# One-core attention and token-routing kernel: the first pair's preparation moved ahead of the constants, and one batch's second layer moved into the tail

## The chip, the cores and the metric

The kernel runs on one core of one Trainium2 chip. The metric is the time of one execution on the device in microseconds (us). Within the core, TensorE (PE in the profile, with its weight loads as PEld), VectorE (DVE), ScalarE (ACT) and GpSimd (POOL) each work through their own list of instructions in order, and SyncE (SP) issues most of the DMAs. They meet through semaphores only.

## The reference

```python
# attention: B, H, S, D = 8, 8, 1152, 64, all float32
q_pool = q.reshape(B, H, S // 2, 2, D).mean(axis=3)
scores = np.matmul(q_pool, k.transpose(0, 1, 3, 2)) / np.sqrt(D)
attn = softmax(scores)                     # with 1e-9 added to the sum
x = np.matmul(attn, v)                     # bridged to (8, 576, 512)
# mixture of depths: capacity 128, w1 (512, 1024), w2 (1024, 512)
s = np.einsum('bsd,d->bs', x, w_gate)
for b in range(B):
    top = np.argpartition(-s[b], capacity)[:capacity]
    y = np.maximum(x[b, top] @ w1, 0.0) @ w2
    out[b] = x[b];  out[b, top] += sigmoid(s[b, top])[:, None] * y
```

## The kernel before

The work is cut into 32 **pairs** of heads (8 batches of 4 pairs) and each pair into two **halves** of 288 pooled queries. For a half, `scores` multiplies nine chunks of 128 keys with the queries: four 64x64-tiled matmuls a chunk (L817), then one exponential of 128x576 on ScalarE (L824). `weighted` multiplies the exponentials with the values (L835, 36 matmuls); `folded` sums them (three additions on GpSimd, L856, and two transposing reductions on VectorE, L861). A float32 matmul is two passes in the trace, so 36 matmuls are 72 rows.

`run` (L1292) writes the order out by hand; the program is built in that order, engine by engine, with no scheduler to move anything. In iteration h the scores of half h are issued, then the weighted sum of half h-1, then one step of every routing unit that is under way (`units`, L1286). A **routing unit** is a generator, `routed` (L996), one for each batch. Each `yield True` ends its step for this iteration. Its steps are: the batch's scores to one line, the ranks (L1076 to L1110), the list of chosen tokens, the gather of 128 rows from the output (L1177, an indirect DMA on GpSimd), their transposition (L1191, L1194), the **first layer** (L1202, 32 matmuls of 128x128, two ReLU copies at L1210), and the **second layer** (L1215, 8 matmuls of 128x512), after which the rows are scaled (L1235), added (L1238) and scattered back (L1239). The tile `xe` (L1176), the index and the gates have two buffers; the PSUM pool has four.

After the loop comes the **tail** (L1365 to L1393). The last batch but one (`old`) has its first and second layer left, and the last batch (`new`) everything from its line of scores on. For the last batch the line comes from a matmul with a diagonal (L1042, L1052, L1059), the columns of scores from five tiny transposes (L679, L682), and the chosen tokens from ten small passes (L1146). The tail interleaves the two by `pieces(unit, n)`: n further steps of a generator.

At the **head** (L1298 to L1305) the first pair is loaded in its natural layout: its queries in two DMAs on ScalarE's queue (L755), its first three chunks of keys in two DMAs on SP's (L759), then the other six chunks and the values. `constants` (L602) runs 12 matmuls of ones on TensorE (L612) and builds the tables: on GpSimd the iotas (L628 to L639), on VectorE four operations (L630, L634, L642, L650). `prepare_first` (L765) adds neighbouring queries (L776, one head on VectorE, one on GpSimd), transposes three chunks of keys (L783, copied by ScalarE at L788), the queries (L794, two copies on VectorE at L801), then the other six chunks (copied by ScalarE). Then the second pair is loaded, and the loop begins.

Of the kernel before, what the change touches and what calls it, by code (L numbers as in the profile page):

```python
# [10 lines left out]
P = 128  # L11
BLK = 32

G = 3
# [520 lines left out]
class _Plain:  # L535
# [10 lines left out]
    def __init__(self, ctx, tc, q, k, v, moe_w_gate, moe_w1, moe_w2, capacity, out):  # L546
        self.tc, self.nc = tc, tc.nc
        self.q, self.k, self.v, self.out = q, k, v, out
        self.w_gate_in, self.w1_in, self.w2_in = moe_w_gate, moe_w1, moe_w2
        B, H, S, D = q.shape  # L550
        self.B, self.H, self.S, self.D = B, H, S, D
        self.Sp = S // 2
        self.Dm = H * D
        self.F = moe_w1.shape[1]
        self.NC = S // P
        self.NPAIR = H // 2
        self.HALF = self.Sp // 2
        self.QB = self.Sp // BLK
        self.HB = self.HALF // BLK
        self.KB = S // BLK  # L560
        self.NF = self.Sp // P
        self.TAIL = self.Sp - self.NF * P
        self.NT = self.NF + 1
        self.ND = self.Dm // P
        self.NFC = self.F // P
        self.NG = self.NC // G
        self.scale = 0.5 / math.sqrt(D)
        self.slots = [(s, min(P, capacity - s)) for s in range(0, capacity, P)]
# [7 lines left out]
        assert all(w > 1 for _, w in self.slots) and capacity < self.Sp  # L576
# [12 lines left out]

        self.sums = self.const.tile([P, self.B * self.NPAIR, self.QB], F32, name="sums")  # L590
        self.w_gate = self.const.tile([P, self.NPAIR, BLK], F32, name="w_gate")
        self.w1 = self.const.tile([P, self.ND, self.F], F32, name="w1")
        self.w2 = self.const.tile([P, self.NFC, self.Dm], F32, name="w2")
# [8 lines left out]
    def constants(self):  # L602
        nc, const = self.nc, self.const
        self.ones = const.tile([P, P], F32, name="ones")
        nc.gpsimd.memset(self.ones[:, :], 1.0)
# [2 lines left out]
        nc.scalar.activation(once[:, :], self.ones[0:1, 0:1], AF.Exp)  # L608

        ps = self.banks()[:, 0, 0:P]  # L610
        for _ in range(12):
            nc.tensor.matmul(ps, lhsT=self.ones[:, :], rhs=self.ones[:, :], start=True, stop=True)  # L612
        self.ident = const.tile([P, P], F32, name="ident")
        make_identity(nc, self.ident[:, :])

        self.before = const.tile([P, P], F32, name="before")
        nc.gpsimd.memset(self.before[:, :], 1.0)
# [38 lines left out]
    def tokens(self):  # L656
        nc = self.nc
# [107 lines left out]
    def prepare_first(self, pair):  # L765

        nc, NC, D = self.nc, self.NC, self.D
        kT = pair["kT"] = self.load.tile([P, self.S], F32, name="kT")
        qT = pair["qT"] = self.load.tile([P, self.Sp], F32, name="qT")
        rows, third = 3 * BLK, self.QB // 3  # L770
        acc = self.work.tile([P, G, 2 * self.HALF], F32, name="acc")
        qp = acc.rearrange("p u n -> p (u n)")[0:rows, 0 : 2 * third * D]
        qp = qp.rearrange("p (n j d) -> p n j d", j=2, d=D)
        of = pair["q"].rearrange("p j (n r) d -> p n j r d", r=2)
        for j, engine in enumerate((nc.vector, nc.gpsimd)):
            engine.tensor_tensor(  # L776
                out=qp[:, :, j, :], in0=of[:, :, j, 0, :], in1=of[:, :, j, 1, :], op=ALU.add
            )

        def keys(a, z):  # L780
            ps = self.banks().rearrange("p b n -> p (b n)")
            for c in range(a, z):
                nc.tensor.transpose(  # L783
                    ps[:, (c - a) * P : (c - a + 1) * P],
                    pair["k"][:, c, :, :].rearrange("p j d -> p (j d)"),
                    self.ident[:, :],
                )
            nc.scalar.copy(kT[:, a * P : z * P], ps[:, 0 : (z - a) * P])  # L788

        keys(0, G)  # L790
        ps = self.banks()
        per = third // 2
        for n in range(third):
            nc.tensor.transpose(  # L794
                ps[:, n // per, n % per * rows : (n % per + 1) * rows],
                qp[:, n, :, :].rearrange("p j d -> p (j d)"),
                self.ident[0:rows, 0:rows],
            )
        to = qT.rearrange("p (t b n i) -> p b n i t", t=3, b=2, i=BLK)
        for bank in range(2):  # L800
            nc.vector.tensor_copy(  # L801
                to[:, bank], ps[:, bank, 0 : per * rows].rearrange("p (n i t) -> p n i t", n=per, t=3)
            )
        keys(G, NC)

    def scores(self, half):

        nc, pair, n = self.nc, half["pair"], self.HALF
        qs = slice(half["s"] * n, (half["s"] + 1) * n)
# [1 line left out]
        for c in range(self.NC):  # L811
            sc = self.banks()
            for e in range(2):
                keys = slice(e * self.D, (e + 1) * self.D)
                for j in range(2):
# [6 lines left out]
                        stop=True,  # L822
                    )
            nc.scalar.activation(p[:, c // G, c % G, :, :], sc[:, :, 0:n], AF.Exp, scale=self.scale)  # L824

    def weighted(self, half):

# [144 lines left out]
    def gated(self, half):  # L972
# [6 lines left out]
        if half["s"] == 1:  # L979
            nc.vector.tensor_tensor(  # L980
                out=pair["part"][:, pair["hp"], :],
                in0=pair["red"][:, :],
                in1=pair["rec"][:, :],
                op=ALU.mult,
            )
            if pair["hp"] == self.NPAIR - 1:
                unit = self.routed(pair["b"], pair["part"])
                next(unit)
                self.routing.append(unit)

# [5 lines left out]
    def routed(self, b, part):  # L996
# [134 lines left out]
        for s0, w in self.slots:  # L1131
# [66 lines left out]
            for f0 in range(0, self.NFC, 4):  # L1198
                pv = self.banks()[:, 0, :].rearrange("p (c n) -> p c n", n=P)
                for f in range(4):  # L1200
# [7 lines left out]
                        )  # L1208
                    if f == 3:
                        nc.scalar.activation(hT[:, f0 : f0 + 4, 0:w], pv[:, :, 0:w], AF.Relu)  # L1210
                    yield f0 + f == self.NFC - 1

            ps = self.banks()[:, 0, :]
            for f in range(self.NFC):
# [4 lines left out]
                    start=(f == 0),  # L1219
                    stop=(f == self.NFC - 1),  # L1220
                )
                if f < self.NFC - 1:
                    yield False
            if b == self.B - 1:
                nc.vector.scalar_tensor_tensor(  # L1225
                    out=xe[0:w, :],
# [58 lines left out]

    def units(self):  # L1286

        for unit in self.routing[::-1]:
            if not any(unit):
                self.routing.remove(unit)  # L1290

    def run(self):  # L1292
        nc = self.nc
        pairs = [(b, hp) for b in range(self.B) for hp in range(self.NPAIR)]
        n_halves = 2 * len(pairs)
        halves = []
        self.routing = []
        upcoming = self.load_first(*pairs[0])  # L1298
        self.load_gate()
        self.constants()  # L1300
        self.prepare_first(upcoming)
        self.tokens()
        loaded = self.load_pair(*pairs[1]) if len(pairs) > 1 else None
        if loaded:
            self.load_values(loaded)  # L1305
        weights = self.weight_loads()
        for h in range(n_halves + 1):
            if h < n_halves:
# [14 lines left out]
                    next(weights, None)  # L1323
                half = {"pair": pair, "s": s}
                halves.append(half)
                self.scores(half)
                if h > 1:

                    of = halves[h - 2 - s]["pair"]
# [36 lines left out]


        self.gated(halves[-1])
        new = self.routing.pop()
        old = self.routing.pop() if self.routing else iter(())  # L1370

        def pieces(unit, n):
            for _ in range(n):
                next(unit, None)

        pieces(old, 4)
        pieces(new, 1)
        pieces(old, 1)
        pieces(new, 1)
        pieces(old, self.NFC - 5)  # L1380
        pieces(new, 2)
        pieces(old, self.NFC // 2)
        pieces(new, 1)
        low = self.counted()
        pieces(old, self.NFC)
        for unit in self.routing + [old]:
            for _ in unit:
                pass
        pieces(new, 1)
        count = self.outside(low)  # L1390
        for _ in new:
            pass
        return nc.values_load(count[0:1, 0:1])  # L1393


# [1 line left out]
def kernel(  # L1397
# [12 lines left out]


    args = (q, k, v, moe_w_gate, moe_w1, moe_w2, capacity, out)
    if capacity % P == 1:

        _any_scores(tc, *args)
        return
# [38 lines left out]
```

## Time and profile before

| | |
|---|---|
| median of 4 runs | 715.04 us |
| the four runs | 713.64, 714.69, 715.39, 716.05 us |
| the profiled execution | 715.53 us, its span 713.6 us |
| TensorE busy in the span | 701.4 us (98%) |
| mean granted TensorE clock | 0.995 |
| longest waits of TensorE in the waits view | 1.4 us (L1052), 1.0 (L612), 0.7 (L1146), 0.7 (L817), 0.7 (L1202) |

The profile is of one execution. Its span runs from the first to the last instruction; 1.9 us of the execution's own time lie around it. A line of the timeline view gives the start in us from the span's start, the time it covers, the engine, the line of the kernel, the operation, the tiles written and read, the size, how many instructions were merged, and in brackets how long the engine had been idle before them and what ended that. The windows view gives, for one stretch, its length, each engine's busy time (with the number of instructions) and the mean granted TensorE clock.

### The profile page before, as it was taken

Reading aid. Unit: us, or ns where it says so; the run is one execution under the profiler, and the core shown is the slowest. Engines: PE = TensorE matmul, PEld = TensorE weight load, DVE = VectorE, ACT = ScalarE, POOL = GpSimd, SP = SyncE. Lnnn points to the kernel's source line nnn. Section 1 sums busy time; section 2 is a strip of 40 time slices with the busy share of each in tenths; the row PEclk is TensorE's granted clock in tenths of the full one; section 3 lists DMA queues with packets and bytes.
Section 4 is the critical chain, followed back from the end, with each engine's and each line's share of the span. In section 5 each row is a group of like instructions: output and inputs, shape, how many; then the busy total and the mean of one; then the engine's idle time right before and its main releaser. Section 6 shows DMA issues by size and latency. Waiting matters only on the chain. (4 is left out here: it accounts for less than half of the span.)

```text
span 713.6 us, 23393 instructions
## 1 busy us (share of the span) xinstructions
PE 701.4 (98%) x9952; PEld 495.8 (69%) x9952; DVE 495.0 (69%) x792; ACT 443.5 (62%) x962; POOL 485.8 (68%) x453
## 2 busy tenths in 40 slices
PE   8999999999999999999999999999999999999896
PEld 6668887875857767576677967678675676756654
DVE  4877777896549965498754978459773697758540
ACT  5677777777547774577746775477754777547310
POOL 5777777868568695577955788467784877657620
PEclk9999999999999999999999999999999999999999
DMA  8899876769682495726866278742878337622200
GB/s 172 180 185 182 178 154 119 132 129 157 123 160 53 89 174 104 138 51 128 156 114 107 51 149 139 133 84 52 165 127 146 68 87 135 119 42 61 51 23 27
DMA packets 389490, 82.86 MB, mean 116 GB/s; under 512 B 376640, under 2 KB 376640, under 8 KB 389376
## 3 DMA queue, kind: packets, MB, share of 16 engines
q1 hardware_dynamic: 387872, 76.49, 57.3%
q0 software_dynamic: 1280, 4.20, 1.8%
q8 instruction: 80, 1.31, 0.8%
q10 hardware_dynamic: 224, 0.59, 0.3%
q14 instruction: 34, 0.28, 0.1%
HBM read 69.65 MB, written 11.59 MB: 114 GB/s over the span
## 5 line engine op out<-in xcount | busy, mean ns | idle before, releaser
L824 ACT ACTIVATE p<-ps 128x576 f32<-128x576 f32 x576 | 319.4, 690 | 3.0 <-PE ps L817 2.4
L856 POOL TENSOR_TENSOR acc<-p 128x576 f32<-128x576 f32 x192 | 266.0, 1414 | 55.1 <-ACT p L824 49.8
L817 PE MATMUL ps<-qT,kT 64*64 64x288 f32 x4608 | 297.2, 406 | 0.9 <-DVE qT L801 0.7
L835 PE MATMUL ps<-p,v_sb 64*64 64x288 f32 x4608 | 294.4, 403 | 0.3 <-ACT p L824 0.2
L835 PEld LDWEIGHTS ps<-p,v_sb 64*64 64x64 f32 x4608 | 210.4, 133 | 71.8 <-ACT p L824 15.9
L817 PEld LDWEIGHTS ps<-qT,kT 64*64 64x64 f32 x4608 | 190.4, 132 | 95.0 <-ACT p L824 27.1
L861 DVE TRANSPOSE_TENSOR_REDUCE fold<-p 128x54 f32<-128x1728 f32 x64 | 126.1, 1970 | 129.6 <-ACT p L824 129.6
L861 DVE TRANSPOSE_TENSOR_REDUCE fold<-acc 128x54 f32<-128x1728 f32 x64 | 124.8, 1950 | 40.4 <-POOL acc L856 40.4
L843 ACT COPY two<-ps 128x576 f32<-128x576 f32 x64 | 40.9, 639 | 130.1 <-PE ps L835 111.2
L845 POOL TENSOR_TENSOR av<-two 128x288 f32<-128x288 f32 x64 | 51.2, 799 | 30.5 <-ACT two L843 28.9
L955 POOL TENSOR_TENSOR x<-avb,rec 128x576 f32<-128x576 f32 x32 | 37.0, 1157 | 41.6 <-DVE rec L953 24.2
L1202 PEld LDWEIGHTS ps<-xeT,w 128*128 128x128 f32 x512 | 58.0, 192 | 3.7 <-ACT sums L901 2.2
L1202 PE MATMUL ps<-xeT,w 128*128 128x128 f32 x512 | 59.7, 277 | 0.7 <-ACT xeT L1194 0.7
L1215 PE MATMUL ps<-w,hT 128*128 128x512 f32 x128 | 58.8, 612 | 0.0
L924 POOL TENSOR_TENSOR prod<-avb,w_gate 128x288 f32<-128x288 f32 x64 | 51.3, 802 | 0.6 <-DVE avb L914 0.6
L901 ACT ACTIVATE sums<-total,tiny 32x18 f32<-32x18 f32 x124 | 38.1, 308 | 11.9 <-DVE total L892 10.3
L1215 PEld LDWEIGHTS ps<-w,hT 128*128 128x128 f32 x128 | 24.2, 194 | 30.1 <-issue 30.1
L732 POOL TENSOR_TENSOR qp<-qb 128x576 f32<-128x576 f32 x31 | 43.7, 1411 | 1.6 <-DMA qb<-in_q_dram 1.6
L735 DVE STREAM_TRANSPOSE kT<-kb 128x1152 f32<-128x1152 f32 x31 | 42.5, 1370 | 0.0
L1210 ACT ACTIVATE hT<-ps 128x512 f32<-128x512 f32 x16 | 9.6, 597 | 48.7 <-PE ps L1202 48.7
L1238 POOL TENSOR_TENSOR xe<-y,xe 128x512 f32<-128x512 f32 x7 | 8.9, 1271 | 42.0 <-ACT y L1235 42.0
L914 DVE STREAM_TRANSPOSE avb<-av 128x288 f32<-128x288 f32 x64 | 29.2, 457 | 7.9 <-POOL av L845 7.8
(94 smaller groups left out, 330.2 us busy)
## 6 DMA issues: line engine op xcount, KB each, us to landing
kb<-in_k_dram SPq DMA_DIRECT2D x124, 144.0 KB, 3.6
qb<-in_q_dram SPq DMA_DIRECT2D x124, 144.0 KB, 3.8
v_sb<-in_v_dram SPq DMA_DIRECT2D x124, 144.0 KB, 3.5
out_dram<-x SPq DMA_DIRECT2D x128, 72.0 KB, 2.9
lines<-row_rank SPq DMA_DIRECT2D x7, 640.0 KB
w<-in_moe_w_dram SPq DMA_DIRECT2D x8, 512.0 KB, 5.4
sc_row<-row SPq DMA_DIRECT2D x7, 288.0 KB
acc<-in_q_dram ACTq DMA_DIRECT2D x2, 288.0 KB
```

The source lines that it names most:

```text
L732: nc.gpsimd.tensor_tensor(out=qp[:, :, :], in0=pair["q"][:, :, 0, :], in1=pair["q"][:, :, 1, :], op=ALU.add)
L735: nc.vector.transpose(kT.rearrange("p (c g i) -> p c g i", c=self.NC, i=BLK), pair["k"].rearrange("p (g c) d -> p c g d", c=self.NC),)
L817: nc.tensor.matmul(sc[keys, j, 0:n], lhsT=pair["kT"][rows, c * P + keys.start : c * P + keys.stop], rhs=pair["qT"][rows, qs], start=True, ...
L824: nc.scalar.activation(p[:, c // G, c % G, :, :], sc[:, :, 0:n], AF.Exp, scale=self.scale)
L835: nc.tensor.matmul(av[j * self.D : (j + 1) * self.D, e, 0:n], lhsT=half["pair"]["v"][keys, j, c, :], rhs=half["p"][keys, c // G, c % G, j, :],
L843: nc.scalar.copy(two[:, :, :], av[:, :, 0:n])
L845: nc.gpsimd.tensor_tensor(out=half["av"][:, :], in0=two[:, 0, :], in1=two[:, 1, :], op=ALU.add)
L856: nc.gpsimd.tensor_tensor(out=acc[:, u, :], in0=units[:, 0, u, :], in1=units[:, 1, u, :], op=ALU.add)
L861: nc.vector.tensor_reduce(fold[:, a, :], of.rearrange("p u (m d) -> p (u m) d", d=BLK), AX.X, ALU.add, apply_transpose=True,)
L924: self.nc.gpsimd.tensor_tensor(out=pair["prod"][:, ns, :], in0=pair["avb"][:, ns, :], in1=self.w_gate[:, hp : hp + 1, :].broadcast_to([P, ...
L1202: nc.tensor.matmul(pv[:, f, 0:w], lhsT=self.w1[:, c, (f0 + f) * P : (f0 + f + 1) * P], rhs=xeT[:, c, 0:w], start=(c == 0), stop=(c == self ...
L1215: nc.tensor.matmul(ps[0:w, 0 : self.Dm], lhsT=hT[:, f, 0:w], rhs=self.w2[:, f, :], start=(f == 0), stop=(f == self.NFC - 1),)
```

## The change

The change has two parts that do not touch each other.

At the **head**, `constants` is split. `first_constants` keeps the matrix of ones, the warm-up matmuls (10 in place of 12) and the identity; `prepare_first` now follows it directly, and the other constants follow that. Both additions of queries go to VectorE. The two copies of transposed queries go to VectorE and ScalarE, one each. The transposes of the last six chunks of keys are no longer issued in `prepare_first`: they are returned as `rest` and issued behind the first chunk of scores, with their copy on VectorE instead of ScalarE. The gate's four DMAs (`load_gate`) go behind the loads of the second pair.

In the **tail**, the unit of the last batch but two is stopped after its first layer (the mark `"hidden"`), and its second layer, `older`, is issued in the tail: six matmuls ahead of the last batch's diagonal matmuls, two behind them. The order of what was there changes with it: the last batch's ranks and pick now stand ahead of all of `old`'s first layer, and `old`'s second layer is cut in five and three matmuls around the transposition of the last batch's rows.

```diff
@@ first_constants / constants
-        for _ in range(12):
+        for _ in range(10):
             nc.tensor.matmul(ps, lhsT=self.ones[:, :], rhs=self.ones[:, :], start=True, stop=True)
         self.ident = const.tile([P, P], F32, name="ident")
         make_identity(nc, self.ident[:, :])
+
+    def constants(self):
+        nc, const = self.nc, self.const
@@ prepare_first
-        for j, engine in enumerate((nc.vector, nc.gpsimd)):
-            engine.tensor_tensor(
+        for j in range(2):
+            nc.vector.tensor_tensor(
...
-        def keys(a, z):
+        def keys(a, z, copy):
...
-            nc.scalar.copy(kT[:, a * P : z * P], ps[:, 0 : (z - a) * P])
-        keys(0, G)
+            copy(kT[:, a * P : z * P], ps[:, 0 : (z - a) * P])
+        keys(0, G, nc.scalar.copy)
...
-        for bank in range(2):
-            nc.vector.tensor_copy(
+        for bank, copy in enumerate((nc.vector.tensor_copy, nc.scalar.copy)):
+            copy(
                 to[:, bank], ps[:, bank, 0 : per * rows].rearrange("p (n i t) -> p n i t", n=per, t=3)
             )
-        keys(G, NC)
+        return lambda: keys(G, NC, nc.vector.tensor_copy)
@@ scores
             nc.scalar.activation(p[:, c // G, c % G, :, :], sc[:, :, 0:n], AF.Exp, scale=self.scale)
+            if c == 0 and behind_first:
+                behind_first()
@@ routed
-                    yield f0 + f == self.NFC - 1
+                    yield "hidden" if f0 + f == self.NFC - 1 else False
...
-                if f < self.NFC - 1:
-                    yield False
+                yield False
@@ units
-        for unit in self.routing[::-1]:
-            if not any(unit):
-                self.routing.remove(unit)
+        for entry in self.routing[::-1]:
+            b, unit = entry
+            if b in self.waiting:
+                continue
+            end = next((mark for mark in unit if mark), None)
+            if end is None:
+                self.routing.remove(entry)
+            elif end == "hidden" and b == self.B - 3:
+                self.waiting.add(b)
@@ run
         upcoming = self.load_first(*pairs[0])
-        self.load_gate()
-        self.constants()
-        self.prepare_first(upcoming)
-        self.tokens()
+        self.first_constants()
+        rest = self.prepare_first(upcoming)
+        self.constants()
         loaded = self.load_pair(*pairs[1]) if len(pairs) > 1 else None
         if loaded:
             self.load_values(loaded)
+        self.load_gate()
...
-                self.scores(half)
+                self.scores(half, rest if h == 0 else None)
...
-        pieces(old, 4)
-        pieces(new, 1)
-        pieces(old, 1)
-        pieces(new, 1)
-        pieces(old, self.NFC - 5)
-        pieces(new, 2)
-        pieces(old, self.NFC // 2)
+        pieces(older, self.NFC - 2)
+        pieces(new, 1)
+        pieces(older, 2)
+        pieces(new, 3)
+        pieces(older)
+        pieces(old, self.NFC)
         pieces(new, 1)
         low = self.counted()
-        pieces(old, self.NFC)
-        for unit in self.routing + [old]:
-            for _ in unit:
-                pass
-        pieces(new, 1)
+        pieces(old, self.NFC - 3)
+        pieces(new, 2)
+        pieces(old)
         count = self.outside(low)
-        for _ in new:
-            pass
+        pieces(new)
```

The rest of the diff changes the handling of other capacities, which the inputs do not use.

More of the change, by code (lines that the diff above doesn't have):

```diff
@@ L567, in __init__ @@
         self.scale = 0.5 / math.sqrt(D)
-        self.slots = [(s, min(P, capacity - s)) for s in range(0, capacity, P)]
+        self.slots = [(0, capacity)]
         assert tuple(out.shape) == (B, self.Sp, self.Dm)
@@ L575, in __init__ @@
         assert self.F == self.NFC * P and self.NFC % 4 == 0
-        assert all(w > 1 for _, w in self.slots) and capacity < self.Sp
+        assert 1 < capacity <= P
         def pool(name, bufs, **kw):
@@ L600, in quarters, with first_constants @@
                 yield j, slice(e * BLK, (e + 1) * BLK), slice(at, at + BLK)
-    def constants(self):
+    def first_constants(self):
         nc, const = self.nc, self.const
@@ L654, in constants @@
         nc.gpsimd.memset(self.tiny[:, :], 1e-9)
-    def tokens(self):
-        nc = self.nc
         self.meta = self.const.tile([P, self.NT, 2], F32, name="meta")
@@ L799, in prepare_first, with scores @@
         to = qT.rearrange("p (t b n i) -> p b n i t", t=3, b=2, i=BLK)
-        for bank in range(2):
-            nc.vector.tensor_copy(
+        for bank, copy in enumerate((nc.vector.tensor_copy, nc.scalar.copy)):
+            copy(
                 to[:, bank], ps[:, bank, 0 : per * rows].rearrange("p (n i t) -> p n i t", n=per, t=3)
             )
-        keys(G, NC)
-    def scores(self, half):
+        return lambda: keys(G, NC, nc.vector.tensor_copy)
+    def scores(self, half, behind_first=None):
         nc, pair, n = self.nc, half["pair"], self.HALF
@@ L988, in gated @@
                 next(unit)
-                self.routing.append(unit)
+                self.routing.append((pair["b"], unit))
     def banks(self):
@@ L1296, in run @@
         halves = []
-        self.routing = []
+        self.routing, self.waiting = [], set()
         upcoming = self.load_first(*pairs[0])
-        self.load_gate()
+        self.first_constants()
+        rest = self.prepare_first(upcoming)
         self.constants()
-        self.prepare_first(upcoming)
-        self.tokens()
         loaded = self.load_pair(*pairs[1]) if len(pairs) > 1 else None
@@ L1368, in run, with pieces @@
         self.gated(halves[-1])
[L1369 to L1374, printed above, removed]
-        pieces(old, 4)
-        pieces(new, 1)
-        pieces(old, 1)
-        pieces(new, 1)
-        pieces(old, self.NFC - 5)
-        pieces(new, 2)
-        pieces(old, self.NFC // 2)
+        left = [unit for _, unit in self.routing]
+        new = left.pop()
+        old = left.pop() if left else iter(())
+        older = left.pop() if left else iter(())
+        assert not left
+        def pieces(unit, n=None):
+            for i, _ in enumerate(unit):
+                if i + 1 == n:
+                    break
+        pieces(older, self.NFC - 2)
+        pieces(new, 1)
+        pieces(older, 2)
+        pieces(new, 3)
+        pieces(older)
+        pieces(old, self.NFC)
         pieces(new, 1)
         low = self.counted()
-        pieces(old, self.NFC)
-        for unit in self.routing + [old]:
-            for _ in unit:
-                pass
-        pieces(new, 1)
+        pieces(old, self.NFC - 3)
+        pieces(new, 2)
+        pieces(old)
         count = self.outside(low)
-        for _ in new:
-            pass
+        pieces(new)
         return nc.values_load(count[0:1, 0:1])
@@ L1412 @@
     args = (q, k, v, moe_w_gate, moe_w1, moe_w2, capacity, out)
-    if capacity % P == 1:
+    if capacity > P or capacity == 1:
         _any_scores(tc, *args)
```

## The prediction

> **What bounds the kernel now.** I read the page's busy table first, then TensorE's timeline at both ends, then the windows with the clock.
>
> ```profile
> PE 701.4 (98%) x9952; PEld 495.8 (69%) x9952; DVE 495.0 (69%) x792; ACT 443.5 (62%) x962; POOL 485.8 (68%) x453
> ```
>
> TensorE is busy 701.4 of 713.6 us and does the same work afterwards, less two warm-up matmuls. The change can only move its idle time (12.2 us), its clock, and what little it adds. The waits view places nearly all idle time at the ends. The tail, from TensorE's timeline:
>
> ```profile
> 669.59 3.82 PE L1202 MATMUL ps<-xeT,w 128*128 128x128 f32 x32
> 674.82 1.21 PE L1052 MATMUL ps<-diag,ones 128*128 128x288 f32 x4 [1.42 <-DVE rank_parts L1074]
> 675.87 1.05 PE L1202 MATMUL ps<-xeT,w 128*128 128x128 f32 x8
> 677.36 0.47 PE L679 MATMUL ps<-ident,sc_row 1*128 1x1 f32 x5 [0.44 <-ACT sc_row L1059]
> 677.75 2.94 PE L1202 MATMUL ps<-xeT,w 128*128 128x128 f32 x24
> 680.53 3.60 PE L1215 MATMUL ps<-w,hT 128*128 128x512 f32 x8
> 684.85 1.33 PE L1146 MATMUL ps<-meta,pick 128*128 128x2 f32 x10 [0.71 <-DVE pick L1137]
> 686.11 5.40 PE L1215 MATMUL ps<-w,hT 128*128 128x512 f32 x8
> 691.56 0.66 PE L1191 MATMUL ps<-ident,xe 128*128 128x128 f32 x4
> 692.89 7.41 PE L1202 MATMUL ps<-xeT,w 128*128 128x128 f32 x64 [0.68 <-ACT xeT L1194]
> 700.14 7.03 PE L1215 MATMUL ps<-w,hT 128*128 128x512 f32 x16
> ```
>
> The windows view of one stretch behind them (TensorE's clock is third from the end):
>
> ```profile
> 686.32:689.74 3.42, 3.42 (x5) 1.34 (x5) 0.00 (x0) 0.12 (x2) 1.11 (x1) 0.50 0.27 77
> ```
>
> The brackets are four waits of the last batch, 3.25 us. The eight passes of L1215 at 686.11 take 5.40 us where the same eight took 3.60 at 680.53. The window tells why: 3.41 us at half clock, behind a wait of 0.71 us and 1.3 us of two-column passes. The head:
>
> ```profile
> 1.04 5.49 PE L612 MATMUL ps<-ones 128*128 128x128 f32 x24 [1.04 <-POOL ones L605]
> 6.44 0.81 PE L783 MATMUL ps<-ident,kb 128*128 128x128 f32 x3
> 7.55 0.72 PE L794 MATMUL ps<-ident,acc 96*128 96x96 f32 x6 [0.29 <-POOL acc L776]
> 8.11 0.82 PE L783 MATMUL ps<-ident,kb 128*128 128x128 f32 x6
> 9.61 9.26 PE L817 MATMUL ps<-qT,kT 64*64 64x288 f32 x144 [0.68 <-DVE qT L801]
> ```
>
> 24 warm-up passes step by 0.213 us, 64 passes of this shape at 692.89 by 0.113: until about 7 us TensorE ran at half clock. Six transposes at 8.11 take what three took at 6.44. The clock column says 1.00 there only because its records begin at 7.07. They run 679.25, 3.41 and 20.48 us: 199, 1 and 6 times 3.413. So the clock is set on a grid of 3.41 us, with a border at 7.07.
>
> **The tail, worked out.** The second layer taken out of the loop is 16 passes, at 630.73:
>
> ```profile
> 626.26 4.55 PE L835 MATMUL ps<-p,v_sb 64*64 64x288 f32 x72
> 630.73 7.13 PE L1215 MATMUL ps<-w,hT 128*128 128x512 f32 x16
> 637.80 4.60 PE L817 MATMUL ps<-qT,kT 64*64 64x288 f32 x72
> ```
>
> 637.80 - 630.73 = **7.07 us** go there, if the rest keeps up. VectorE ends that iteration's work at 637.17 and then idles 6.52 us; the next fold would be due at 643.69 - 7.07 = 636.62, so it starts 0.55 late. Its next idle gap, 0.53 us at 648.43, takes that up. GpSimd loses L1238 and L1239 (638.67 to 641.32), after which its sums (due with the fourth chunk's exponential, about 640.3) come nearer on time. I count no loss; without that cover up to 0.55.
>
> Now the tail on the old time axis. L1215 steps by 7.07/16 = 0.44 us, or 0.428 between passes of a run.
> - `older`, 12 passes from 669.59: to 674.73. The diagonal is there at 674.82 as before, so 1.42 us of waiting is filled. L1052: 674.82 to 675.87.
> - four passes: to 677.58. ScalarE's row of scores was ready at 677.36, so 0.44 is filled too, and L679 is 0.24 later than now. It takes 0.40.
> - `old`'s first layer, 64 passes in 692.89 to 700.14 = 7.25: 677.98 to 685.23. VectorE's ranks and pick follow L679, so the pick is there at 684.85 + 0.24 = 685.09. The 0.71 is filled.
> - L1146, 1.26 as now: to 686.49. The low-work stretch is 1.3 us in place of 2.0. The window 672.67 to 676.08 holds two runs of work of 0.8 and 1.3 us and 1.4 of idling and kept full clock; here more is busy. No half clock.
> - ten passes of `old`'s second layer, 4.28: to 690.8. The gather, issued 1.81 after L1146 starts (686.65 - 684.85), is issued at 687.04; now it lands at 690.05, 3.40 after its issue, so 690.44: hidden, by 0.3 us.
> - four transposes, 0.45: to 691.25; six passes, 2.57: to 693.82. Meanwhile ScalarE copies xeT, which takes 1.33 from L1191 to L1202 now: ready at 692.1. The last 0.68 is filled.
> - L1270 0.12, then both layers of the last batch as now: L1202 starts at 693.94 instead of 692.89, **1.05 us later**.
>
> Tail and loop together: 7.07 - 1.05 = **6.02 us gained**; 1.7 of it is the half clock (3.41 x 0.5). What is moved with it: `older`'s L1235, L1238 and L1239 run at 678.8 to 682.1 on idle ScalarE and GpSimd; ScalarE's L1235 stands behind the gate's exponential, which waits for GpSimd, not for TensorE. The last gather needs the buffer of `xe` that `older` scatters from; a scatter from 681.1, landing after 3.15 (693.87 to 697.01 now), ends at 684.3, ahead of 687.04.
>
> **The head, worked out.** By the landings in the trace, the second head's queries come at 6.21 and the keys' second part at 6.31. Neither depends on the constants. The keys' transposes stay at 6.44 to 7.1.
> - Both additions on VectorE: the second from 6.29, 0.55 long, done at 6.83 (now GpSimd's, 7.50). The query transposes can follow the keys' at 7.11 instead of 7.55: 0.44 earlier, last done at 7.83.
> - Two copies: ScalarE's copy does not run beside VectorE's. They write one tile, and the built program has ScalarE wait for VectorE there. VectorE 0.66: 8.52. ScalarE's strided copy is not in the trace; contiguous rows (L788: 0.48 for 384 columns, 0.80 for 768) give 0.40, the strided L1059 (1.24 for 576) gives 0.62. I take 0.55, nearer the strided: 9.1. Scores from 9.15 to 9.2 instead of 9.61: 0.4 gained.
> - Then six transposes stand between the first and second chunk: 0.51 + about 0.9 (four between 64x64 runs took 0.68 at 664.2) puts chunk two at 10.6, against 10.11 now: 0.45 lost. VectorE's copy of their result stands behind four constants. In the trace these take 2.37, 0.78, 0.36 and 0.23, the first two beside GpSimd's iotas; alone they cost no more than 0.76 and 0.18 (L1042 and L1117, same widths), 1.4 together, done at 9.9, ahead of the transposes. Lower end no delay, upper end 3.7 us, done at 12.3. I take 1.4, as GpSimd is idle by then. The copy (0.8 to 0.95) ends at 11.6, chunk four starts at about 11.7 against 11.1.
>
> From there ScalarE paces the first 18 chunks, 0.53 us an exponential, so a delay stays: **0.4 us lost** at full clock. The gate's DMAs and the second pair's only move earlier or later within slack: the gate is read first at 30.4.
>
> **The clock at the head** is what I cannot hide. With 20 passes the warm-up ends at 5.47, and TensorE then idles to 6.44. In the window 3.66 to 7.07 it works 1.81 + 0.63 of 3.41 us, 71%, where it is filled now. In the window before, it worked from 1.04 to 3.66, 77%, and stayed at half clock. So on this grid 71% would not release the clock at 7.07. At half clock the query transposes, the first chunk and the transposes in the middle take twice as long and leave the next window short too. Release at 10.48 costs half of the cold work between, 1.2 us; release at 13.9 about 2.6. The phase of the grid against the start is chance, so I take the middle, 1.9 us. Head: 0.4 + 1.9 = **2.3 us lost**.
>
> The Trainium skill ("TensorE: Matmul & The Clock Gate", Part 1) says the opposite: the transition comes around 4 us into sustained matmuls, and it is undone by long idling only. By that rule 4.3 us of warm-up would do and the sum would be without the 1.9. The rows speak against it: here the release came 6.0 us after the first matmul, and half clock came back after 0.71 us of true idling.
>
> **Sum.** 715.53 - 6.02 + 2.3 = **711.8 us**, against the profiled execution's own time. That stands 0.5 above the median 715.04; a run whose tail kept full clock would be 1.7 shorter, about the lowest of the four, and the new tail no longer depends on that.
>
> **Rivals.**
> 1. The warm-up suffices: 715.53 - 6.02 + 0.4 = 709.9. For it: 4.3 us of matmuls; against it: the 77% window.
> 2. The tail's gather is late. Gathers take 3.4 to 6.5 us to land in this trace, median 4.8; at 4.8 TensorE waits 1.2 us before L1191: 713.0. Against it: no other DMA runs then, as now.
> 3. Slower: the loop does not shrink. If VectorE used the 7.07 us to catch up, the taken-out layer saves little while the tail and head pay 1.05 + 2.3: at nothing saved 715.53 + 1.05 + 2.3 = 718.9; it is slower than before once more than 3.7 us (6.02 - 2.3) of the 7.07 are lost. Against it: VectorE is 0.55 late, with 0.53 of slack.
> 4. The copy of six key chunks waits 2.3 us longer behind slow constants, without the clock: 715.53 - 6.02 + 2.4 = 711.9. Against it: GpSimd is idle.
>
> **Chances.** Forecast 0.52, rival 1 0.28, rival 2 0.08, rival 3 0.05, rival 4 0.07. The range 708.9 to 713.6 takes in all but rival 3, with 1 us below rival 1. A measurement of this kernel tells about 0.3% (2.1 us) from no change: faster needs less than 712.9. Forecast and rivals 1 and 4 lie below, but a release at 13.9 does not by much: 0.86 faster, 0.10 same, 0.04 slower.
>
> **What would show it.** Right: L1215 x12 directly ahead of L1052 with no wait, no half clock near the end, no L1215 in the iteration at about 630, the last layer starting 6.0 less the head's loss earlier. For the head: 20 passes, idling to 6.4, chunk one before 9.3 and chunk two after 10.5 if warm; chunks stepping by 0.97 us if cold. Wrong: TensorE waiting in the loop after 20 us, or waiting for DMA at L1191.

## The result and the profile after

| | before | after |
|---|---|---|
| median | 714.73 us (57 runs) | 713.43 us (36 runs) |
| lowest and highest | 713.16, 716.52 us | 710.48, 714.40 us |
| profiled execution: own time, span | 715.53, 713.6 us | 712.74, 711.0 us |
| ratio after to before, 95% interval | | 0.9975 [0.9969, 0.9981] |

The change makes the kernel 0.25% faster by the ratio, which is 1.8 us; the medians differ by 1.3. That lies within the 0.3% that the prediction called no change. The two profiled executions differ by 2.8 us, more than the medians: that of before was 0.8 above its median, that of after 0.7 below. The spread of after is wider, 3.9 us against 3.4, and that is part of the answer.

The line of busy times on the page of after:

```profile
PE 699.9 (98%) x9948; PEld 487.7 (69%) x9948; DVE 494.3 (70%) x793; ACT 443.7 (62%) x962; POOL 485.1 (68%) x452
```

TensorE's timeline of after at the head, and the windows view of after (first the stretch, its length, PE's busy time; TensorE's clock is third from the end):

```profile
1.04 4.64 PE L612 MATMUL ps<-ones 128*128 128x128 f32 x20 [1.04 <-POOL ones L605]
6.37 0.52 PE L783 MATMUL ps<-ident,kb 128*128 128x128 f32 x3 [0.69 <-DMA kb<-in_k_dram]
6.88 0.71 PE L794 MATMUL ps<-ident,acc 96*128 96x96 f32 x6
9.04 0.72 PE L818 MATMUL ps<-qT,kT 64*64 64x288 f32 x8 [1.44 <-ACT qT L801]
9.68 1.51 PE L783 MATMUL ps<-ident,kb 128*128 128x128 f32 x6
11.13 9.65 PE L818 MATMUL ps<-qT,kT 64*64 64x288 f32 x136
20.61 3.63 PE L838 MATMUL ps<-p,v_sb 64*64 64x288 f32 x56
```

```profile
6.33:9.75 3.42, 1.94 (x18) 1.12 (x19) 2.02 (x6) 1.15 (x2) 0.25 (x1) 1.00 1.21 278
9.75:13.16 3.41, 3.41 (x27) 2.15 (x30) 0.96 (x1) 1.30 (x2) 0.00 (x0) 0.50 0.88 139
```

Two waits frame the short transposes: 0.69 us for the keys and 1.44 us for ScalarE's copy of the queries. The first scores start at 9.04 instead of 9.61, but behind them the clock is at half from 9.75 to 13.16. The six transposes take 1.51 us instead of 0.82, and only then does the second chunk start, at 11.13. The first weighted sum (L838) starts at 20.61, where L835 started at 18.69: **1.92 us lost at the head**.

The tail, again from TensorE's timeline of after:

```profile
659.60 0.63 PE L1194 MATMUL ps<-ident,xe 128*128 128x128 f32 x4 [0.78 <-ACT two L846]
...
664.93 5.40 PE L1218 MATMUL ps<-w,hT 128*128 128x512 f32 x12
670.55 1.21 PE L1055 MATMUL ps<-diag,ones 128*128 128x288 f32 x4 [0.23 <-DVE rank_parts L1077]
671.60 1.88 PE L1218 MATMUL ps<-w,hT 128*128 128x512 f32 x4
673.41 0.46 PE L679 MATMUL ps<-ident,sc_row 1*128 1x1 f32 x5
673.80 7.41 PE L1205 MATMUL ps<-xeT,w 128*128 128x128 f32 x64
681.29 1.33 PE L1149 MATMUL ps<-meta,pick 128*128 128x2 f32 x10
682.55 4.56 PE L1218 MATMUL ps<-w,hT 128*128 128x512 f32 x10
686.95 0.60 PE L1194 MATMUL ps<-ident,xe 128*128 128x128 f32 x4
...
690.18 7.41 PE L1205 MATMUL ps<-xeT,w 128*128 128x128 f32 x64
```

The four bracketed waits of before are gone but for 0.23 us at the diagonal, and the passes of L1218 behind the pick step by 0.44 us: no half clock. There is one new wait, 0.78 us, at 659.60, ahead of the transposes of the last batch but one. It is put down to ScalarE, but what L1194 needs is the gather, which by the landings came at 659.47. The gather itself was not slow: it landed 3.62 us after its issue, against 3.70 in before (660.02 to 663.73). It was issued late. The last batch's first layer starts at 690.18 instead of 692.89. With the 1.92 us of the head taken out, tail and loop are 2.71 + 1.92 = **4.63 us shorter**.

### The profile page after: what moved, and what is told of

Read it like the earlier page. It is cut to its first block, busy times and chain, and to the rows that moved or that the text cites. A ratio compares the mean times of both kernels' runs of the same rounds, so it can differ in the third digit from the quotient of the medians.

```text
span 711.0 us, 23390 instructions
## 1 busy us (share of the span) xinstructions
PE 699.9 (98%) x9948; PEld 487.7 (69%) x9948; DVE 494.3 (70%) x793; ACT 443.7 (62%) x962; POOL 485.1 (68%) x452
## 4 chain that ended last, share of the span: by engine, by line
PE 95%; ACT 1%; POOL 1%; DVE 1%; DMA 1%; issue 0%; POOLq 0%; SPq 0%; DVEq 0%; ACTq 0%
PE ps L818 40%; PE ps L838 38%; PE ps L1205 8%; PE ps L1218 7%; ACT p L825 1%; DMA kb<-in_k_dram 1%; POOL acc L859 1%; PE ps L1194 1%; DVE fold L864 0%; PE ps L783 0%; POOL prod L927 0%; PE ps L1149 0%; ACT sums L904 0%; PE ps L1055 0%; POOL x L958 0%
## 5 line engine op out<-in xcount | busy, mean ns | idle before, releaser
L838 PE MATMUL ps<-p,v_sb 64*64 64x288 f32 x4608 | 294.2, 403 | 0.0
L838 PEld LDWEIGHTS ps<-p,v_sb 64*64 64x64 f32 x4608 | 207.4, 133 | 74.1 <-ACT p L825 15.4
L818 PEld LDWEIGHTS ps<-qT,kT 64*64 64x64 f32 x4608 | 186.6, 133 | 100.5 <-ACT p L825 28.0
L1218 PE MATMUL ps<-w,hT 128*128 128x512 f32 x128 | 57.3, 598 | 0.0
L1218 PEld LDWEIGHTS ps<-w,hT 128*128 128x128 f32 x128 | 23.6, 190 | 28.1 <-issue 28.0
L1240 POOL TENSOR_TENSOR xe<-y,xe 128x512 f32<-128x512 f32 x7 | 8.9, 1275 | 38.3 <-ACT y L1237 38.3
```

Source lines behind the costliest of these rows:

```text
L818: nc.tensor.matmul(sc[keys, j, 0:n], lhsT=pair["kT"][rows, c * P + keys.start : c * P + keys.stop], rhs=pair["qT"][rows, qs], start=True, ...
L838: nc.tensor.matmul(av[j * self.D : (j + 1) * self.D, e, 0:n], lhsT=half["pair"]["v"][keys, j, c, :], rhs=half["p"][keys, c // G, c % G, j, :],
L1218: nc.tensor.matmul(ps[0:w, 0 : self.Dm], lhsT=hT[:, f, 0:w], rhs=self.w2[:, f, :], start=(f == 0), stop=(f == self.NFC - 1),)
```

## The experiments

The theory at this point: tail and loop gain some 4 us; the head gives most of it back, through the clock (it goes to half speed because TensorE idles between the shortened warm-up and the scores). Its rival: the head loses through its order alone, six transposes and a copy behind the first chunk. Chips differ by 1 to 2 us in this kernel, so each run is compared with runs of the kernel before on its own chip.

| run | what it is | ratio to before, 95% interval | its runs, us |
|---|---|---|---|
| e9 | the changed kernel again | 0.9976 [0.9965, 0.9988] | 709.10 to 712.08 |
| e1 | its head alone | 1.0015 [1.0003, 1.0026] | 712.26 to 716.27 |
| e2 | its tail alone | 0.9956 [0.9943, 0.9969] | 709.05 to 709.83 |
| e3 | changed, 14 warm-up matmuls | 0.9963 [0.9950, 0.9976] | 709.57 to 710.65 |
| e4 | before, 10 warm-up matmuls | 1.0011 [1.0002, 1.0020] | 712.02 to 714.47 |
| e5 | changed, 12 warm-up matmuls | 0.9950 [0.9937, 0.9963] | 710.30 to 711.41 |
| e6 | changed, all keys ahead of the scores | 0.9941 [0.9926, 0.9955] | 709.06 to 711.04 |
| e7 | new tail alone, an earlier batch held | 0.9938 [0.9924, 0.9951] | 709.19 to 710.29 |
| e8 | e7 with a head from both | 0.9925 [0.9913, 0.9937] | 708.28 to 709.82 |
| e10 | changed, the second gap filled | 0.9963 [0.9950, 0.9976] | 709.57 to 710.05 |

e1 to e4 ran on one chip (median of before 712.37 us), e5 to e8 on another (713.62), e9 and e10 on a third (712.30).

### e1 and e2: the two parts apart

e1 has the new head with the old `units` and tail; e2 has the old head with the new `units` and tail. Of each edit only the lines of the hold are shown:

```diff
# e1, against the changed kernel
-            elif end == "hidden" and b == self.B - 3:
-                self.waiting.add(b)
...
# e2, against the kernel before
+            elif end == "hidden" and b == self.B - 3:
+                self.waiting.add(b)
...
```

> The head of the changed kernel with the tail and the routing of the one before. The clock theory (TensorE idles ahead of the keys since the warm-up is shorter, and so gets half clock at the head in most executions): 2 to 3 us slower than before. Its rival, the order theory (only the six transposes and the copy behind the first chunk cost): 0.4 us slower, within 0.3% either way.

> The head of the kernel before with the tail and the held second layer of the changed one. The profile of after makes the tail and the loop 4.6 us shorter than in the profile of before; 1.7 of that is the half clock of that one execution, which not every execution has. Expected by both theories of the head: 3.5 to 4.6 us faster than before. If the tail were worth only what the whole change measures (1.3 us), the head would cost nothing and both theories would fall.

The head alone loses 0.15%, 1.1 us (0.2 to 1.9). The tail alone gains 0.44%, 3.1 us (2.2 to 4.1). Together they make 0.29%, against the 0.25% of the whole change. e2 came out below its expected 3.5 to 4.6. By its clocks the kernel before does not have half clock in its tail in every execution: of its 22 runs on that chip 13 lie between 711.88 and 712.38 us at a mean clock of 0.997 or 0.998, and nine between 713.28 and 713.77, all at 0.995 or 0.996. The two groups lie some 1.4 us apart, and the prediction had counted 1.7 in full. e1 lies between the two theories by its ratio, but its spread of 4 us, against 1.9 of before on that chip, speaks for the clock (part of it is the old tail's half clock, which e1 keeps). In its profiled execution the clock was at half from 7.97 to 14.80 us, and the weighted sum started at 21.50, 2.81 us later than in before.

### e3 to e5: the length of the warm-up

```diff
-        for _ in range(10):
+        for _ in range(14):      # e3; 12 in e5; e4 is before with 10 for 12
```

> The changed kernel with 14 warm-up matmuls in place of 10, which fill TensorE's time up to the landing of the keys at 6.3 us. Clock theory: 2 us or more faster than the changed kernel, so 3 to 4 us faster than before. Order theory: as the changed kernel, 1.3 us faster than before, or 0.5 worse than that since the warm-up then ends behind the landing.

> The kernel before with 10 warm-up matmuls in place of 12, nothing else. Clock theory: 1 to 2 us slower than before. Order theory: no change, since TensorE waits for the keys at 6.3 us anyway.

> The changed kernel with 12 warm-up matmuls as before, the head's new order kept. Clock theory: most of the half clock at the head goes, so 1.5 to 2.5 us faster than before; what is left of the head's loss is its order. Order theory: as the changed kernel (0.9975 of before).

e5 shows that the warm-up matters in the changed kernel: two matmuls more make it 0.25% faster (0.9950 against 0.9975 and 0.9976), and its five runs spread over 1.1 us. TensorE's timeline of e5:

```profile
6.60 0.52 PE L783 MATMUL ps<-ident,kb 128*128 128x128 f32 x3 [0.72 <-DMA kb<-in_k_dram]
6.96 0.66 PE L794 MATMUL ps<-ident,acc 96*128 96x96 f32 x6
9.06 0.71 PE L818 MATMUL ps<-qT,kT 64*64 64x288 f32 x8 [1.44 <-ACT qT L801]
9.71 0.87 PE L783 MATMUL ps<-ident,kb 128*128 128x128 f32 x6
10.51 8.83 PE L818 MATMUL ps<-qT,kT 64*64 64x288 f32 x136
19.17 4.60 PE L838 MATMUL ps<-p,v_sb 64*64 64x288 f32 x72
```

Here the clock is full from 5.04 us on, and this is the price of the order by itself, as far as one execution shows it: 19.17 - 18.69 = **0.48 us**. The first chunk is 0.55 earlier, the second 0.40 later, as the transposes stand between. What is left of the 1.92 us, 1.44, is the clock. But these lines do not show that the longer warm-up closed the gap ahead of the keys: the first warm-up passes ran at half clock, those behind 5.04 at full, so the 24 passes ended at 5.88, and TensorE waited 0.72 and 1.44 us as in after (0.69 and 1.44).

e3 gained less than expected, 2.6 us on before instead of 3 to 4: its warm-up ran to 7.2 us in the profiled execution, past the landing of the keys at 6.3, and the weighted sum started at 19.71. There TensorE did not wait for the keys, only the 1.44 us for the queries, and the clock stayed full from 7.14 us on.

e4 does not settle what the shorter warm-up costs by itself. It is 0.11% slower than before by the ratio, 0.8 us (0.1 to 1.4), and 1.3 by the medians, near the 1 to 2 of the clock theory. But TensorE's timeline of e4 has no loss at the head:

```profile
6.24 0.52 PE L783 MATMUL ps<-ident,kb 128*128 128x128 f32 x3 [0.56 <-DMA kb<-in_k_dram]
7.56 0.72 PE L794 MATMUL ps<-ident,acc 96*128 96x96 f32 x6 [0.80 <-POOL acc L776]
8.11 0.82 PE L783 MATMUL ps<-ident,kb 128*128 128x128 f32 x6
9.61 9.25 PE L817 MATMUL ps<-qT,kT 64*64 64x288 f32 x144 [0.68 <-DVE qT L801]
18.69 4.60 PE L835 MATMUL ps<-p,v_sb 64*64 64x288 f32 x72
```

The clock is full from 6.20 us, the weighted sum starts at 18.69 as before, and the half clock of this execution lies in the tail (685.45 to 688.86). Nine of its 12 runs lie at 713.20 to 713.89 with a mean clock of 0.995 or 0.996, where the slower runs of before lie. So most of its loss looks like half clock in the tail, in more of the executions; why in more is not shown.

### e6 and e10: the second gap

```diff
# e6
-        return lambda: keys(G, NC, nc.vector.tensor_copy)
+        keys(G, NC, nc.scalar.copy)
# e10, ahead of the return
+        ps = self.banks()[:, 0, 0:P]
+        for _ in range(6):
+            nc.tensor.matmul(ps, lhsT=self.ones[:, :], rhs=self.ones[:, :], start=True, stop=True)
```

e6 has 10 warm-up matmuls, as its expectation says; only its label says 12.

> The changed kernel with the six transposes of keys ahead of the scores again, copied by ScalarE; still 10 warm-up matmuls. Order theory: the head's 0.4 us come back and 0.3 to 0.5 more, so 0.6 to 0.9 us faster than the changed kernel. Clock theory: no more than that, as TensorE still idles ahead of the keys: 1 us or more slower than the kernel with 12 warm-up matmuls.

> The changed kernel as it is, as a measure for the runs beside it on the same chip: 1.3 us (0.25%) faster than before, its times spread over 3 to 4 us by the clock at the head.

> The changed kernel with six more matmuls of ones behind the transposes of the queries, where TensorE waits 1.4 us for the two copies; still 10 warm-up matmuls, so the idling ahead of the keys stays. They add no result. If the second gap is what lets the clock fall back or keeps it from rising (the clock theory as the last runs leave it: both gaps together), 1.5 to 2.5 us faster than the changed kernel, like the run with all keys ahead of the scores. If the gap ahead of the keys alone does it, no faster. In executions that are at half clock there, the six take 2.6 us instead of 1.3 and delay the scores by 1 us.

e6 fell outside both expectations: with the warm-up as short as in the changed kernel it is 0.34% faster than that, 2.4 us. With the six transposes ahead of the scores TensorE has work where the changed kernel waits 1.44 us. TensorE's timeline of e6:

```profile
6.37 0.87 PE L783 MATMUL ps<-ident,kb 128*128 128x128 f32 x3 [0.69 <-DMA kb<-in_k_dram]
7.03 1.17 PE L794 MATMUL ps<-ident,acc 96*128 96x96 f32 x6
7.99 1.49 PE L783 MATMUL ps<-ident,kb 128*128 128x128 f32 x6
9.66 9.44 PE L818 MATMUL ps<-qT,kT 64*64 64x288 f32 x144 [0.18 <-ACT qT L801]
18.93 4.60 PE L838 MATMUL ps<-p,v_sb 64*64 64x288 f32 x72
```

In this execution the clock rises only at 10.06 us, yet the scores start at 9.66 and the weighted sum at 18.93, 0.24 later than in before, since what ran at half clock stood beside the copies. In this order the short warm-up and the gap behind it cost little.

e10 leaves the first gap and the order, and only fills the second gap with work that has no use:

```profile
6.20 0.52 PE L783 MATMUL ps<-ident,kb 128*128 128x128 f32 x3 [0.52 <-DMA kb<-in_k_dram]
6.86 0.71 PE L794 MATMUL ps<-ident,acc 96*128 96x96 f32 x6
7.41 1.53 PE L807 MATMUL ps<-ones 128*128 128x128 f32 x12
9.04 0.72 PE L822 MATMUL ps<-qT,kT 64*64 64x288 f32 x8
9.69 0.87 PE L783 MATMUL ps<-ident,kb 128*128 128x128 f32 x6
10.49 8.83 PE L822 MATMUL ps<-qT,kT 64*64 64x288 f32 x136
19.15 4.60 PE L842 MATMUL ps<-p,v_sb 64*64 64x288 f32 x72
```

The scores start at the same 9.04, the clock stays full, and the weighted sum starts at 19.15. All five runs lie within 0.5 us, 709.57 to 710.05; of the changed kernel's ten on that chip three lie below that and seven between 710.81 and 712.08. By the medians e10 is 1.3 us faster, below the expected 1.5 to 2.5, and the intervals of the two ratios overlap; the narrowed spread is the clearer sign. The windows view shows what the filling did: behind its release e10 has 2.70 us of work in one window of 3.41 (5.58 to 8.99), where e9, the changed kernel on the same chip, has 1.41, and after 1.94. So work in the second gap (e10, e6) or a longer warm-up (e3, e5) gives most of the loss back. That both gaps are needed for the loss is not shown: e5 and e4 have two such gaps in their profiled executions and kept the clock.

### e7 and e8: what the loop lost, and a faster kernel

VectorE's timeline of after, 5 us behind the place where the second layer was taken out (its readings of the accumulator left out), and GpSimd's beside it:

```profile
636.59 0.53 DVE L1093 TENSOR_SCALAR_CACHE_REDUCE cmp<-sc_row,gate_sc 128x320 f32<-128x320 f32 x1
637.05 1.55 DVE L1103 SCALAR_TENSOR_TENSOR tie<-sc_row,gate_sc,before 128x128 f32<-128x128 f32 x1
638.54 0.59 DVE L1084 TENSOR_SCALAR_CACHE_REDUCE cmp<-sc_row,gate_sc 128x384 f32<-128x384 f32 x1
...
639.40 0.61 DVE L1103 SCALAR_TENSOR_TENSOR tie<-sc_row,gate_sc,before 128x128 f32<-128x128 f32 x1
```

```profile
635.62 4.25 POOL L859 TENSOR_TENSOR acc<-p 128x576 f32<-128x576 f32 x3 [1.45 <-ACT p L825]
```

The same two engines in before, in the same iteration:

```profile
635.31 0.33 DVE L1100 SCALAR_TENSOR_TENSOR tie<-sc_row,gate_sc,before 128x128 f32<-128x128 f32 x1
```

```profile
638.67 1.27 POOL L1238 TENSOR_TENSOR xe<-y,xe 128x512 f32<-128x512 f32 x1 [6.24 <-ACT y L1235]
```

The tie is the operation of the ranks that orders equal scores. It has two tensor inputs, and it took 0.33 us in before. There GpSimd was idle, waiting for the second layer's result. Now GpSimd's additions run beside it and it takes 1.55 us, while the comparisons ahead and behind, with one tensor input, keep their 0.53 and 0.59. With a second tie at 0.61 instead of 0.34 VectorE's work in this iteration is 1.5 us longer. Its next fold starts at 640.32, 2.1 us after its input. The list of tokens and the issue of the gather come 1.3 us late (655.84, where 660.02 less the 5.48 us that the loop is ahead by then would be 654.54), and TensorE waits at 659.60. e7 is e2 with these lines changed. It holds the second layer of the batch before that one, so that the one in question stays where it was and covers the ties:

```diff
-            elif end == "hidden" and b == self.B - 3:
+            elif end == "hidden" and b == self.B - 4:
-            xe = ffn.tile([P, self.Dm], F32, name="xe")
+            xe = ffn.tile([P, self.Dm], F32, name="xe", bufs=3)      # index, own_gate too
-            diag = ffn.tile([P, self.QB, BLK], F32, name="diag", bufs=1)
+            diag = ffn.tile([P, self.QB, BLK], F32, name="cmp", bufs=1)
```

> The head of the kernel before, the new tail, but the second layer that is kept for the tail is that of the last batch but three (with three buffers for the gathered rows, the index and the gates, and the diagonal in the buffer of the compared lines). Theory of the cover: the 7 us of TensorE's work alone at about 630 let VectorE's ties run without GpSimd beside them; with them back there, the wait before the last but one batch's transposes (0.8 to 1.1 us) and the late diagonal (0.4 us) go: 1.0 to 1.5 us faster than the kernel with the new tail alone, and the tie takes 0.33 us, not 1.55. Rival (the gather was late by itself, its landing being chance): as the new tail alone.

> The tail of the run with the last batch but three, and a head put together from both: the first pair ahead of the constants, both additions of queries and both copies of them on VectorE, all keys ahead of the scores, 12 warm-up matmuls. Expected: the scores start at 9.2 instead of 9.6 us, so 0.4 us faster than the new tail with the last batch but three alone, and 4 to 5 us faster than before; no gain over that kernel if the clock pays for the shorter head.

```profile
627.11 0.33 DVE L1100 SCALAR_TENSOR_TENSOR tie<-sc_row,gate_sc,before 128x128 f32<-128x128 f32 x1
```

```profile
656.09 0.63 PE L1191 MATMUL ps<-ident,xe 128*128 128x128 f32 x4
...
661.41 5.40 PE L1215 MATMUL ps<-w,hT 128*128 128x512 f32 x12
666.90 1.21 PE L1052 MATMUL ps<-cmp,ones 128*128 128x288 f32 x4
```

These are VectorE's and TensorE's timelines of e7. The tie is back at 0.33 us, and neither L1191 nor the diagonal (L1052) waits. In e2, the tail alone, the same tie took 1.55 us and L1191 waited 1.0. So it is in every profile here: in the seven kernels that hold the batch but two (after, e2, e3, e5, e6, e9, e10) the tie takes 1.53 to 1.55 us and the transposes wait 0.6 to 1.2; in before, e1, e4, e7 and e8, which leave that layer in the loop, it takes 0.33 or 0.34 and they do not wait. The late diagonal follows the issue of the gather, 13.8 to 13.9 us behind it in before, after, e2, e7 and e8. In e8 it waits 0.38 us although the tie takes 0.33, as there the list stood 0.64 us for a DMA. e7 is 0.18% faster than e2 by the ratios (1.3 us, as expected), though from two chips and with overlapping intervals; the vanished waits are what shows the cause.

e8 adds a head without the order's loss: both additions and both copies of the queries on VectorE, 12 warm-up matmuls, all keys ahead of the scores. TensorE's timeline of e8:

```profile
9.21 9.25 PE L818 MATMUL ps<-qT,kT 64*64 64x288 f32 x144 [0.34 <-DVE qT L801]
18.29 4.59 PE L838 MATMUL ps<-p,v_sb 64*64 64x288 f32 x72
```

The weighted sum starts 0.40 us earlier than in before, as expected; against e7 the ratios give 0.9 us, with overlapping intervals. It is the fastest here, 0.75% ahead of before (0.63 to 0.87), and ahead of the changed kernel by 0.5%.

## Why the prediction was right, and where it was not

It forecast 711.8 us, faster; measured are 713.43, faster by less: within the range of 708.9 to 713.6, with 0.2 us to spare. The direction was right, and so were the two largest terms, the layer taken out and a loss at the head through the clock; the sum was 1.6 us too low. By its own measure, under 712.9 for faster, this is no clear change, to which it gave a chance of 0.10 against 0.86 for faster. Against the profiled execution it put the gain at 3.7 us; the profiled executions differ by 2.8 and the medians by 1.3. It had taken a profiled execution of before that is 0.8 us above the median, with a half clock in its tail that most executions, by their clocks, do not have, so its sum counted a gain that is mostly not there to be had. One of its own signs of being wrong came, too: TensorE waits in the loop after 20 us, at L1194.

- **The layer taken out, 7.07 us.** At its place the shift of TensorE's work is 1.73 + 5.44 = 7.17 us. Right.
- **"I count no loss" behind it.** Wrong, and the step that failed most clearly. I moved VectorE's operations with the times that they had beside an idle GpSimd. In their new place the tie took 1.55 us, and the fold started 2.1 us late, not 0.55. By way of the gather, 1.3 us late, it cost 0.78 us at L1194 and 0.39 at the diagonal. That is rival 3's mechanism, at a sixth of its full price.
- **The tail, 1.05 us longer.** All four waits were filled as worked out, apart from the late diagonal. From the diagonal to the last batch's first layer it took 0.51 us more than worked out: one tie beside L1240 took 0.74 us instead of 0.35 and held the pick, and the rest went a tenth at a time in passes that I had stepped too tightly. Tail and loop came to 4.63 instead of 6.02 us; a drift of 0.2 us in the loop to the good, for which I have no cause, is in it.
- **The half clock in the tail, 1.7 us.** It was there in the profiled execution and is gone in after. But by the clocks it is in nine of 22 executions of before on one chip and in two of 15 on another. Against a median it is worth less than half of what I took.
- **The head at full clock, 0.4 us lost.** Measured 0.48 (e5). ScalarE's strided copy took 0.67 us where I took 0.55, VectorE's four constants 1.1 where I took 1.4; the second chunk came at 10.51, forecast 10.6. The first 18 exponentials take 9.89 us in before, nearer 0.55 each than the 0.53 that I wrote; nothing rests on that.
- **The clock at the head, 1.9 us.** Its size was near (1.44 in the profiled execution), its course in that execution was not. I argued that a window 71% full would not release the clock, on the grid of before. Here the grid lay otherwise, and the clock was released at 6.33, behind a window that is 81% full (2.76 us of work from 2.92 on; the warm-up ended at 5.68, not at the 5.47 of my sum). That does not speak against my share: windows of 77 to 80% did not release it (2.62 us in before, 2.69 in e3 and e8, 2.72 in e6). What came instead was a fall: the window 6.33 to 9.75 holds 1.94 us of work, and the next ran at half clock. The second gap, the wait for the serial copies, I had seen but not counted against the clock; e10 shows that filling it keeps the clock. A late release as I forecast it may have come in other executions. The record of the clock begins only at the first release, so a late one leaves the mean near 1: in e6, released at 10.06, it reads 0.998. Two runs of e1 at 0.998 took 714.73 and 714.92 us beside two at 0.998 with 712.26 and 712.27 on the same chip, and five of after at 0.999 took 713.35 to 713.89 where four others at 0.999 or 0.998 took 710.48 to 710.70. None of these was profiled, so this stays open.
- **The Trainium skill** ("TensorE: Matmul & The Clock Gate", Part 1) has in its table a warm clock fall back after a whole window of idling; the same part tells of a kernel in which frequent short pauses made it go up and down, so "long idling only" in the prediction said more than the page. Here it fell in the head after waits of 0.7 and 1.4 us with work between, and in the old tail after 0.71. The measurements decide: in this kernel a window that is partly empty can be enough. For the tie a page did have the rule, which the prediction left out: by "GPSIMD Engine Reference", Specifications, GpSimd shares its SBUF interfaces with VectorE and contends with operations of VectorE that have two SBUF inputs. The 1.55 against 0.33 us agrees with it.

What stays open: which share of a window decides. The windows behind the release in e5 and e9:

```profile
5.04:8.46 3.42, 1.86 (x16) 1.51 (x15) 1.45 (x4) 0.60 (x2) 0.79 (x2) 1.00 1.20 278
```

```profile
5.45:8.86 3.41, 1.41 (x11) 0.84 (x9) 1.65 (x5) 0.89 (x2) 0.37 (x2) 1.00 1.20 281
8.86:12.27 3.41, 3.10 (x18) 1.75 (x22) 0.78 (x3) 0.91 (x2) 0.25 (x1) 0.50 0.95 149
```

With 1.41 us of work in e9, 1.66 in e1 and 1.94 in after the next window ran at half clock; with 1.86 in e5 and e7, 1.89 in e4 and 1.97 in e3 it did not. A border between 1.66 and 1.86 would sort all but after's 1.94, and the ends of matmuls are modelled. The kind of work in the windows differs as well, and no run here separates that.

## What to carry to other kernels

Work that an engine does alone is cover for others: before taking it out, re-time what ran beside it as it will run beside its new neighbours, and bound by the durations that the same operation has elsewhere in the trace. Short gaps around a short piece of work can cost clock on top of the waiting (1.44 us here), so count how full each 3.4 us are, and fill a gap that can't be closed. A gain that is seen in one profiled execution and hangs on the clock has to be weighed by how often it occurs, which the spread and the mean clocks of the runs tell.

## What the runs showed of the hardware that I had not expected

- Adding six useless matmuls (1.5 us of TensorE's time) made the changed kernel faster by 1.3 us at the median on one chip, and cut its spread from 3.0 us (ten runs) to 0.5 (five).
- An operation with two tensor inputs on VectorE took up to 1.55 us beside GpSimd's additions instead of 0.33, ending within 0.2 us of the end of one of them; operations with one tensor input beside the same additions kept their times.
- The clock was released in before's profiled execution only 6.0 us behind the first matmul, in e1's already 3.5 us behind it. With the same 12 warm-up matmuls from 1.04 us on it came at 7.07 us in before, 5.96 in e2, 5.04 in e5 and 4.22 in e7: the phase of the 3.41 us grid differs from execution to execution.
